# Four normalisations ahead of a weight load on GpSimd, one v load behind w_out, and two w_out jobs swapped, in a sliding-window attention + gated MLP kernel

## The chip, the cores and the metric

One core of one Trainium2 chip runs the whole program. The metric is the device time of one execution in microseconds, as the median over runs; lower is better.

The engines are named as in the profile: PE is TensorE (matmuls; PEld is its weight load), DVE is VectorE, ACT is ScalarE, POOL is GpSimd, SP is SyncE, which only issues DMAs here. POOL issues DMAs too, and each of its requests occupies POOL while the descriptors are written.

## The reference

q, k and v are 8 batches x 8 heads x 576 positions x 64. Attention is causal with a window of 64 positions. Its output, laid out as 4608 tokens x 512, goes through a two-layer network.

```python
def _attn_ref(q, k, v):
    scores = scale * np.matmul(q, k.transpose(0, 1, 3, 2))
    mask = (rel >= 0) & (rel < window)          # rel = query position - key position, window = 64
    scores = np.where(mask, scores, -1000000000.0)
    attn = softmax(scores)
    return np.matmul(attn, v)

def _moe_ref(x, w_in, w_out):                   # x 4608 x 512, w_in 512 x 2048, w_out 2048 x 512
    h = x @ w_in
    g = h * np.cos(h)
    return g @ w_out
```

(The softmax is abridged. Inputs are float32; the kernel loads them as bfloat16 and writes float32.)

## The kernel before

The 4608 tokens are worked on in 9 tiles of 512. Batch 0 fills tile 0 and the first 64 tokens of tile 1, and so on. Per tile there is attention (scores, softmax, transposition of the weights, values), which gives `xT`; then `h = w_in x xT` in 16 blocks, `gT = h * sin(h + pi/2)`, and `out = gT x w_out`. From tile 1 on a planner weaves the attention of later batches into the network of the current tile. Tile 0 and the attention of batch 1 have no earlier network to hide behind: their order is written out by hand, in a string of steps called `FIRST`, and each engine runs its instructions in the order in which the steps were written. The change is in this string alone.

A step is a letter code and arguments. Those that matter here:

- `Lwi.i` and `Lwo.i` load quarter i of w_in and w_out (lines 208 and 211, POOL requests); `Lv1.c` loads chunk c of v of batch 1 (line 192); `Lq1.p`, `Lk1.p` load heads of batch 1, `Lq2.c`, `Lk2.c` chunks of batch 2 (lines 169 and 186).
- Scores are made in groups. For tile 0 a group is (p, g): head pair p, half g of the tile; the groups `G*.8` to `G*.18` are the rest of batch 0 and batch 1. Each group runs `s` (scores on PE), `m` (row maximum on DVE), `e` (exponential with its sum on ACT, line 376), `i` (reciprocal `rden` on DVE, line 386), `n` (normalisation `w = e * rden`, line 393, on POOL unless its letter is `d`), and `w` (transposition on PE, line 409) with `c` (copy of the transposed weights to `wT`). For batch 1, `Gc` is the transposition by a DMA that SP issues (line 412), `Gw` the one on PE.
- `zA`, `zB`, `zC` spread v of batch 0 to the in-between block positions: `zA` on DVE, `zB` and `zC` as DMAs of SP (line 203). `yA`, `yB` do it for batch 1 on POOL, and `y.1.d` on DVE.
- `v.a.g` are the value matmuls of two head pairs for half g (line 446), `x` their copy to `xT`, `h.g.f` the w_in matmuls of two blocks for half g (line 460), `V.p` and `X.p` the same two steps of tile 1 (line 428).
- `o.j.m` multiplies the four blocks of w_out's quarter j into output block m of tile 0 (line 479): four matmuls, one job. `oc.m` copies the finished output block out of PSUM.

An `h.g.f` with f = 2, 3 reads w_in's second quarter (`Lwi.1`), f = 4, 5 the third (`Lwi.2`), f = 6, 7 the fourth. All requests of POOL go through one software DMA queue.

Of the kernel before, what the change touches and what calls it, by code (L numbers as in the profile page):

```python
# [10 lines left out]
def _safe_warn(msg, *a, **kw):  # L11
# [37 lines left out]


FIRST = (
# [19 lines left out]
)  # L71


# [713 lines left out]
```

## Time and profile before

| | us |
|---|---|
| median of 3 runs (297.42 to 297.9) | 297.88 |
| the profiled execution, its own time | 296.92 |
| its span, first to last instruction | 295.2 |
| PE busy in the span | 285.3 (97%) |
| ACT, DVE, POOL busy | 238.0, 230.3, 209.7 |
| software DMA queue: packets' time as a share of 16 engines' span | 83.5% |

Something of 1.72 us lies around the span in the profiled execution, and the median of the runs is 0.96 us above that execution. TensorE's granted clock is 1.000 throughout. Since PE is busy 97% of the span, what counts is where PE stands still, and which wait ends last there. Times in the timeline rows are microseconds from the start of the span: start, duration, engine, line, operation, count, and in brackets the idle time ahead of it with what ended it.

### The profile page before, as it was taken

To read this page: it belongs to the slowest core of one execution; us is meant where nothing else is said; L and a number is where in the kernel's file an instruction comes from. 1 tells how busy PE (TensorE), PEld (TensorE's weight loads), DVE (VectorE), ACT (ScalarE), POOL (GpSimd) and SP (SyncE) were. 2 spreads that over 40 slices of the span, in tenths; PEclk is the share of its full clock that TensorE was granted. 3 is DMA by queue.
4 is the path that set the end of the run, shared out by engine and by line. 5 is a ranking of instruction groups with operands and counts; after the bars stand their busy time and mean duration, and the time that the engine had idled before them with its cause. 6 is when DMAs were issued, how large, how long until landed. Compare 5 with 4: busy or idle time off the path is not lost.

```text
span 295.2 us, 8262 instructions
## 1 busy us (share of the span) xinstructions
PE 285.3 (97%) x2786; PEld 163.2 (55%) x2815; DVE 230.3 (78%) x906; ACT 238.0 (81%) x791; POOL 209.7 (71%) x230
## 2 busy tenths in 40 slices
PE   8979999999999999999999999999999999999995
PEld 3668854544454444444454545444547854884595
DVE  4998888887887876788678876996689878957853
ACT  5998699888987798879987999799977896937710
POOL 9999568992899759984999399948995476133200
PEclk9999999999999999999999999999999999999999
DMA  7999999999999999999999999999959415042013
GB/s 149 174 201 205 196 191 143 141 143 155 203 197 120 162 235 154 155 163 232 168 142 158 235 155 145 147 213 185 141 122 200 45 38 178 2 117 83 0 38 107
DMA packets 168267, 43.81 MB, mean 148 GB/s; under 512 B 155616, under 2 KB 163872, under 8 KB 168224
## 3 DMA queue, kind: packets, MB, share of 16 engines
q0 software_dynamic: 100896, 18.06, 83.5%
q1 hardware_dynamic: 67184, 25.15, 46.7%
q8 instruction: 22, 0.36, 0.5%
q14 instruction: 21, 0.17, 0.2%
q10 hardware_dynamic: 144, 0.07, 0.1%
HBM read 36.70 MB, written 9.44 MB: 156 GB/s over the span
## 4 chain that ended last, share of the span: by engine, by line
PE 86%; POOL 5%; ACT 3%; DMA 2%; issue 2%; DVE 1%; POOLq 0%
PE h_ps L496 38%; PE out_ps L747 18%; PE out_ps L585 13%; PE h_ps L460 5%; PE out_ps L479 5%; PE o_ps L428 3%; ACT e L376 2%; PE s_ps L327 2%; DMA wT<-w 2%; POOL v L192 1%; POOL q L169 1%; POOL k L169 1%; POOL w L393 1%; PE tw_ps L409 1%; PE s_ps L349 1%
## 5 line engine op out<-in xcount | busy, mean ns | idle before, releaser
L496 PE MATMUL h_ps<-xT,w_in 128*128 128x512 bf16 x502 | 111.3, 379 | 1.3 <-DVE xT L130 0.8
L393 POOL TENSOR_TENSOR w<-e,rden 128x512 bf16<-128x512 f32 (+1 forms) x68 | 69.2, 1030 | 48.6 <-DVE rden L386 38.6
L734 DVE TENSOR_TENSOR gT<-h_ps,sin 128x512 bf16<-128x512 f32 x128 | 84.6, 687 | 21.8 <-ACT sin L731 20.4
L376 ACT ACTIVATE e<-s,negm 128x128 f32<-128x128 f32 (+1 forms) x256 | 97.2, 382 | 2.6 <-DVE negm L364 1.6
L731 ACT ACTIVATE sin<-h_ps 128x512 f32<-128x512 f32 x128 | 73.6, 599 | 25.4 <-PE h_ps L496 23.5
L496 PEld LDWEIGHTS <-w_in 128*128 128x128 bf16 x512 | 50.2, 98 | 59.3
L747 PE MATMUL out_ps<-w_out,gT 128*128 128x512 bf16 x305 | 68.7, 379 | 1.1 <-issue 0.8
L364 DVE CUSTOM_DVE_ANT_0 s<-s_ps,mask 128x128 f32<-128x128 f32 (+1 forms) x256 | 55.8, 277 | 1.9 <-PE s_ps L349 1.6
L747 PEld LDWEIGHTS <-gT 128*128 128x128 bf16 x320 | 30.4, 98 | 35.5
L376 ACT ACTIVATION_READ_ACCUMULATOR e<-s,negm 128x1 f32 x256 | 48.0, 188 | 0.0
L192 POOL DMA_DIRECT2D v<-in_v_dram x40 | 34.1, 874 | 1.0 <-issue 0.9
L186 POOL DMA_DIRECT2D q<-in_q_dram x30 | 26.3, 894 | 3.6 <-issue 3.0
L186 POOL DMA_DIRECT2D k<-in_k_dram x30 | 26.3, 887 | 0.0
L386 DVE RECIPROCAL rden<-den 128x4 f32<-128x4 f32 (+1 forms) x73 | 12.0, 165 | 17.2 <-ACT e L376 16.8
L130 POOL COPY v<-v 64x1536 bf16<-64x1536 bf16 (+3 forms) x16 | 22.9, 1431 | 0.4
L364 DVE DVE_READ_ACCUMULATOR2_ANT negm<- 128x1 f32 x256 | 21.2, 83 | 0.0
L525 POOL TENSOR_TENSOR qT<-gT 128x512 bf16<-128x512 bf16 x12 | 13.6, 1154 | 9.1 <-DVE gT L734 9.0
L130 DVE CAST xT<-o_ps 128x512 bf16<-128x512 f32 x24 | 15.5, 680 | 5.8 <-PE o_ps L428 5.5
L585 PEld LDWEIGHTS <-gT 128*128 128x128 bf16 x152 | 14.0, 98 | 2.2
L460 PE MATMUL h_ps<-xT,w_in 128*128 128x256 bf16 x128 | 14.6, 273 | 0.0
L479 PE MATMUL out_ps<-w_out,gT 128*128 128x512 bf16 x60 | 14.3, 380 | 0.3 <-issue 0.2
L556 DVE TENSOR_TENSOR out_sb<-out_ps,p 128x512 f32<-128x512 f32 (+2 forms) x16 | 8.6, 548 | 6.7 <-ACT p L130 5.6
(90 smaller groups left out, 327.0 us busy)
## 6 DMA issues: line engine op xcount, KB each, us to landing
out_dram<-out_sb SPq DMA_DIRECT2D x16, 512.0 KB, 8.2
v<-in_v_dram POOLq DMA_DIRECT2D x32, 128.0 KB, 5.8
q<-in_q_dram POOLq DMA_DIRECT2D x24, 128.0 KB, 8.5
k<-in_k_dram POOLq DMA_DIRECT2D x24, 128.0 KB, 7.1
w_in<-in_moe_w_in_dram POOLq DMA_DIRECT2D x4, 512.0 KB, 9.4
w_out<-in_moe_w_out_dram POOLq DMA_DIRECT2D x4, 512.0 KB, 11.0
q<-in_q_dram POOLq DMA_DIRECT2D x7, 144.0 KB, 5.7
k<-in_k_dram POOLq DMA_DIRECT2D x7, 144.0 KB, 5.8
```

What stands on the lines that cost most here:

```text
L130: {"a": nc.scalar.copy, "p": nc.gpsimd.tensor_copy}.get(engine, nc.vector.tensor_copy)(out, in_)
L186: nc.gpsimd.dma_start(out=st[name, b][0:n, c].rearrange("p (h d) -> p h d", h=H), in_=src.rearrange("h p d -> p h d"))
L192: nc.gpsimd.dma_start(out=vt.rearrange("p (h d) -> p h d", h=H), in_=v[b, :, c * 128:c * 128 + n, :].rearrange("h p d -> p h d"))
L364: nc.vector.tensor_tensor_reduce(out=s[:, u, c], in0=s_ps[:, u, c], in1=mask[:, 2 - j % 2 if j else 0, c], scale=-scale if b else -1.0, sc ...
L376: nc.scalar.activation(e[:, u, c], s[:, u, c], AF.Exp, bias=negm[:, u:u + 1], scale=1.0 if n < n_first else -1.0, accum_out=den[:, u:u + 1])
L393: (nc.gpsimd if engine == "p" else nc.vector).tensor_tensor(out=w[:, 0:u], in0=e[:, 0:u], op=ALU.mult, in1=rden[:, 0:u].unsqueeze(2).to_br ...
L460: nc.tensor.matmul(out=h_ps[:, half * e:half * e + half], lhsT=w_in_sb[:, ks, ff * 128:ff * 128 + 128], rhs=st["xT", 0][:, ks, half * g:ha ...
L496: nc.tensor.matmul(out=st["h", ff], lhsT=w_in_sb[:, ks, ff * 128:ff * 128 + 128], rhs=st["xT", mt][:, ks], start=start, stop=stop)
L585: nc.tensor.matmul(out=to[n_] if split else to[:, e], lhsT=lhs[name][f // 2][:, f % 2, 128 * e:128 * e + 128], rhs=rhs[name][:, f, lo:hi], ...
L731: nc.scalar.activation(sin, h_ps, AF.Sin, bias=math.pi / 2.0)
L734: nc.vector.tensor_tensor(out=gt[:, e], in0=h_ps, in1=sin, op=ALU.mult)
L747: nc.tensor.matmul(out=o_ps[e], lhsT=gT[ff // 2][:, ff % 2, ms * 128:ms * 128 + 128], rhs=w_out_sb[:, ff], start=ff == 0, stop=ff == n_ff - 1)
```

## The change

Four edits in the string of steps; no function changes, and after it the file is one line shorter, so that its line numbers are lower by one.

```diff
-e.3.0 Lwi.2 Tk.1 n.1.0.p s.2.1.1 Pq.1.d Gs.10.2 m.2.1 Gs.9.4 n.0.0.p Pk.1.a n.2.0.p i.3.0 e.1.1 w.0.0 zA.0.d w.1.0 c.0.0.d Gs.12.0 w.2.0 n.3.0.p i.0.1 c.1.0.d zA.1.d
+e.3.0 Tk.1 n.1.0.p s.2.1.1 Pq.1.d zA.0.d Gs.10.2 Gs.9.4 n.0.0.p Pk.1.a n.2.0.p e.1.1 w.0.0 w.1.0 c.0.0.d i.3.0 Gs.12.0 w.2.0 n.3.0.p Lwi.2 i.0.1 c.1.0.d m.2.1 zA.1.d
...
-h.1.3.1 Lv1.0 Lwo.1 ... Lwo.3 h.1.7.4 Lv1.1
+h.1.3.1 Lwo.1 ... Lwo.3 h.1.7.4 Lv1.0 Lv1.1
...
-o.0.1.2 Gi.9 o.2.0 ... o.1.1 ... o.3.0 Ge.13 o.2.1 Gi.11 oc.0.d
+o.0.1.2 Gi.9 o.1.1 ... o.2.0 ... o.2.1 Ge.13 o.3.0 Gi.11 oc.0.d
```

1. `Lwi.2` goes from ahead of the norms of tile 0's first half to behind them.
2. On DVE, `zA.0` goes ahead of the maximum `m.2.1`, which moves behind `c.1.0`, and `i.3.0` behind `c.0.0`.
3. `Lv1.0` goes from ahead of `Lwo.1` to behind `Lwo.3`.
4. Of the output jobs, `o.1.1` changes places with `o.2.0`, and `o.2.1` with `o.3.0`: the third and the fourth quarter of w_out are first read one job later.

On POOL, the first norms of tile 0 stand behind the third w_in request before the change (a name in brackets is a semaphore that the instruction waits for; DMASW0 to DMASW7 are eight completion counters that POOL's requests use in turn, so that each request waits for the one eight places ahead of it):

```order
L208 DMA w_in<-in_moe_w_in_dram 128x4x512 [waits DMASW7_49]
L208 DMA w_in<-in_moe_w_in_dram 128x4x512 [waits DMASW0_49]
L393 TENSOR_TENSOR w<-e,rden 128x512 [waits DVE_49,Pool_49]
L393 TENSOR_TENSOR w<-e,rden 128x512
L393 TENSOR_TENSOR w<-e,rden 128x512 [waits DVE_49] x5
L208 DMA w_in<-in_moe_w_in_dram 128x4x512 [waits DMASW1_49]
```

Now the third request (the one on DMASW0) is behind four of them:

```order
L207 DMA w_in<-in_moe_w_in_dram 128x4x512 [waits DMASW7_49]
L392 TENSOR_TENSOR w<-e,rden 128x512 [waits DVE_49,Pool_49]
L392 TENSOR_TENSOR w<-e,rden 128x512
L392 TENSOR_TENSOR w<-e,rden 128x512 [waits DVE_49] x2
L207 DMA w_in<-in_moe_w_in_dram 128x4x512 [waits DMASW0_49]
L392 TENSOR_TENSOR w<-e,rden 128x512 [waits DVE_49] x3
L207 DMA w_in<-in_moe_w_in_dram 128x4x512 [waits DMASW1_49]
```

The four norms moved up by one request; the three behind it did not.

Also on POOL, later, around the w_out requests and up to the first norm of batch 1 (w with 384 columns is group 10), before:

```order
L192 DMA v_78<-in_v_dram 128x8x64 [waits DMASW6_49]
L211 DMA w_out<-in_moe_w_out_dram 128x4x512 [waits DMASW7_49]
L169 DMA k<-in_k_dram 96x2x384 [waits DMASW0_49]
L211 DMA w_out<-in_moe_w_out_dram 128x4x512 [waits DMASW1_49]
L211 DMA w_out<-in_moe_w_out_dram 128x4x512 [waits DMASW2_49]
L192 DMA v_78<-in_v_dram 128x8x64 [waits DMASW3_49]
...
L192 DMA v_77<-in_v_dram 64x8x64 [waits DMASW6_49]
L186 DMA q<-in_q_dram 128x8x64 [waits DMASW7_49,PE_49]
L186 DMA q<-in_q_dram 128x8x64 [waits DMASW0_49]
L186 DMA q<-in_q_dram 128x8x64 [waits DMASW1_49]
L393 TENSOR_TENSOR w<-e,rden 128x384 [waits DVE_49,PE_49,Pool_49]
```

and now:

```order
L210 DMA w_out<-in_moe_w_out_dram 128x4x512 [waits DMASW6_49]
L168 DMA k<-in_k_dram 96x2x384 [waits DMASW7_49]
L210 DMA w_out<-in_moe_w_out_dram 128x4x512 [waits DMASW0_49]
L210 DMA w_out<-in_moe_w_out_dram 128x4x512 [waits DMASW1_49]
L191 DMA v_78<-in_v_dram 128x8x64 [waits DMASW2_49]
...
L191 DMA v_77<-in_v_dram 64x8x64 [waits DMASW6_49]
L185 DMA q<-in_q_dram 128x8x64 [waits DMASW7_49,PE_49]
L185 DMA q<-in_q_dram 128x8x64 [waits DMASW0_49]
L185 DMA q<-in_q_dram 128x8x64 [waits DMASW1_49]
L392 TENSOR_TENSOR w<-e,rden 128x384 [waits DVE_49,PE_49,Pool_49]
```

With the v request gone from ahead of them, the last three w_out requests and the k request moved to the counter before their old one; the q requests stay on DMASW7, 0 and 1. So the counter DMASW1 that the third q request waits for is that of w_out's third quarter before, and of its fourth quarter now.

On DVE, in the first half of tile 0, before:

```order
L130 COPY qT1_76<-tq_ps_386 128x576
L359 TENSOR_REDUCE negm_460<-s_ps_441 128x4
L386 RECIPROCAL rden_476<-den_420 128x4
L130 COPY v0_77<-v0_77 64x512
L130 COPY wT_495<-tw_ps_484 128x512
L386 RECIPROCAL rden_512<-den_348 128x4
L130 COPY wT_514<-tw_ps_490 128x512
```

and now:

```order
L129 COPY qT1_76<-tq_ps_386 128x576
L129 COPY v0_77<-v0_77 64x512
L129 COPY wT_490<-tw_ps_480 128x512
L385 RECIPROCAL rden_492<-den_420 128x4
L385 RECIPROCAL rden_510<-den_348 128x4
L129 COPY wT_512<-tw_ps_485 128x512
L358 TENSOR_REDUCE negm_514<-s_ps_440 128x4
```

The maximum (`m.2.1`) left its place ahead of the first copy of v and stands two copies of `wT` later; the reciprocal of `den_420` (`i.3.0`, for the fourth norm) follows the first copy of `wT`.

37 rows, old and new, of the table FIRST are left out of this document.

## The prediction, before the changed kernel was run

> **What bounds the kernel now.** I read the page's chain of work that ended last, then PE's waits and timeline between 10 and 56 us, where the change lies, and then, for each place where PE could start earlier, the engine or transfer that it would meet next.
>
> ```profile
> span 295.2 us, 8262 instructions
> PE 86%; POOL 5%; ACT 3%; DMA 2%; issue 2%; DVE 1%; POOLq 0%
> PE tw_ps L409 <- POOL w L393: 1.4, 2, 1.1
> ```
>
> PE is most of the chain, so a microsecond counts only if PE stands still for it. In the stretch of the change POOL's norms cost PE 1.4 us in two waits. The rows, with what follows them on PE:
>
> ```profile
> 16.65 0.62 PE L409 MATMUL tw_ps<-ident,w 128*128 128x128 bf16 x8 [1.06 <-POOL w L393]
> 18.73 0.40 PE L409 MATMUL tw_ps<-ident,w 128*128 128x128 bf16 x4 [0.38 <-POOL w L393]
> 24.43 0.44 PE L446 MATMUL o_ps<-wT,v 128*64 128x64 bf16 x16 [0.17 <-issue]
> 26.37 10.65 PE L460 MATMUL h_ps<-xT,w_in 128*128 128x256 bf16 x96
> ```
>
> The norms are late because POOL first writes three w_in requests:
>
> ```profile
> 11.95 1.52 POOL L208 DMA_DIRECT2D w_in<-in_moe_w_in_dram  x2
> 13.74 0.74 POOL L208 DMA_DIRECT2D w_in<-in_moe_w_in_dram  x1 [0.27 <-DVE rden L386]
> 14.55 6.16 POOL L393 TENSOR_TENSOR w<-e,rden 128x512 bf16<-128x512 f32 x6
> 13.42 0.17 DVE L386 RECIPROCAL rden<-den 128x4 f32<-128x4 f32 x1
> 16.42 0.18 DVE L386 RECIPROCAL rden<-den 128x4 f32<-128x4 f32 x1 [0.34 <-ACT e L376]
> 19.54 0.66 ACT L130 CAST xT<-o_ps 128x512 bf16<-128x512 f32 x1
> ```
>
> **Part 1: the third w_in request behind four norms, and the DVE moves.** POOL is free at 11.95 + 1.52 = 13.47, and the first norm's reciprocal ends at 13.42 + 0.17 = 13.59. So the norms start at about 13.65 instead of 14.55: 0.90 us earlier. A norm takes 6.16 / 6 = 1.03 us. The fourth needs i.3.0, whose exponentials bound it to 16.4 (the row that waits for ACT); its new place behind c.0.0 puts it at about 16.5, still ahead of the fourth norm's turn at 13.65 + 3 x 1.03 = 16.75. So PE's two waits would end at about 15.75 and 17.84. The DVE moves cost nothing: zA.0 and c.0.0 are done before 16.75, and m.2.1 feeds exponentials that ACT cannot start before its earlier ones are through. If that cover fails, it is the next exponential that is late, by one row maximum.
>
> At 17.78 POOL writes the third request (0.74 us), and the fifth norm starts at about 18.59, where it started before (14.55 + 4 x 1.03 = 18.67). So the gain is 0.90 us for the first half alone, and ACT's first copy to xT, at 19.54 behind its exponentials, hardly moves. PE then needs what the DMA queue brings. Two kinds of row tell when that is: issue on POOL or SP, and the time from issue to landing. In order: the three w_in requests above (11.95, 12.7, 13.74), then the second SP request that spreads v (zB.1) with its landing:
>
> ```profile
> w_in<-in_moe_w_in_dram POOLq DMA_DIRECT2D x1, 512.0 KB, 8.3
> w_in<-in_moe_w_in_dram POOLq DMA_DIRECT2D x1, 512.0 KB, 10.4
> w_in<-in_moe_w_in_dram POOLq DMA_DIRECT2D x1, 512.0 KB, 12.5
> 18.27 0.84 SPq L203 DMA_DIRECT2D v<-v  x1
> v<-v SPq DMA_DIRECT2D x1, 128.0 KB, 6.1
> ```
>
> The quarters land at 20.25, 23.1 and 26.24, one about every 3.0 us: the queue serves them one after the other and has a backlog, so a request's own issue time doesn't set its landing. The third, issued at 17.78, is still queued 5.3 us before the second lands, and should land at 26.24 as before. Its first reader is the w_in matmul at 26.37. And zB.1 lands at 18.27 + 6.1 = 24.37; the value matmuls at 24.43, with 0.17 us of idle PE that the row calls issue, are v.0.1, which read that spread. PE thus waits for a transfer there already. The front gain of 0.90 us ends at 24.37 at the latest, and at 26.24 once more: I take 0 for what is left, between a bound of 0.1 (26.37 less 26.24) and no loss.
>
> A rule speaks against this move: the Trainium skill, "DMA: Bandwidth & Descriptors", section "Rules for kernel authors", says to issue a DMA early and to wait for it late. Read as landing following issue, the third quarter would come 17.78 - 13.74 = 4.04 us later, at 30.28, and PE would stand 3.9 us, for 301.8. The spacing of the landings contradicts that here; it stays as a rival.
>
> **Part 2: Lv1.0 behind w_out, the swapped jobs, and the counters.** No wait for w_out appears among PE's, so the swapped jobs remove none; they cost nothing as long as the finished block's copy out of PSUM, one job later, is through before its bank's next scores, two jobs on; without that cover the price would be the rest of one copy. What the move of Lv1.0 does change is which transfer POOL's third q request waits for. POOL's requests that wait for a counter show the pattern:
>
> ```profile
> 23.99 0.80 POOL L211 DMA_DIRECT2D w_out<-in_moe_w_out_dram  x1
> w_out<-in_moe_w_out_dram POOLq DMA_DIRECT2D x1, 512.0 KB, 7.7
> 31.94 0.74 POOL L211 DMA_DIRECT2D w_out<-in_moe_w_out_dram  x1 [2.08 <-DMA w_out<-in_moe_w_out_dram]
> 29.09 0.76 POOL L211 DMA_DIRECT2D w_out<-in_moe_w_out_dram  x1
> w_out<-in_moe_w_out_dram POOLq DMA_DIRECT2D x1, 512.0 KB, 12.0
> 41.37 0.88 POOL L186 DMA_DIRECT2D q<-in_q_dram  x1 [0.59 <-DVE negm L364]
> ```
>
> The fourth w_out request, eight behind the first, starts at 31.94, 0.25 us after the first lands (23.99 + 7.7 = 31.69). The third q request starts at 41.37, 0.28 us after w_out's third quarter lands (29.09 + 12.0 = 41.09); the row names DVE, but the order shows only a counter. Now that counter is the fourth quarter's. Its landing:
>
> ```profile
> w_out<-in_moe_w_out_dram POOLq DMA_DIRECT2D x1, 512.0 KB, 11.7
> 26.05 0.63 POOL L169 DMA_DIRECT2D q<-in_q_dram  x1
> q<-in_q_dram POOLq DMA_DIRECT2D x1, 144.0 KB, 7.8
> 26.67 0.92 POOL L192 DMA_DIRECT2D v<-in_v_dram  x1
> v<-in_v_dram POOLq DMA_DIRECT2D x1, 128.0 KB, 8.1
> ```
>
> Issued at 31.94, it lands at 43.64. Lv1.0 took the queue from 26.05 + 7.8 = 33.85 to 26.67 + 8.1 = 34.77, so without it the quarter lands 0.92 us earlier, at 42.72, and the third q request starts at 43.0: 1.63 us later than before. Queued behind it on POOL are all norms of batch 1; who waits for them are PE's transposition of group 8 and SP's DMA transpositions:
>
> ```profile
> 42.26 4.55 POOL L393 TENSOR_TENSOR w<-e,rden 128x384 bf16<-128x384 f32 x5
> 46.75 1.03 POOL L130 COPY v<-v 64x1024 bf16<-64x1024 bf16 x1
> 48.62 1.04 POOL L393 TENSOR_TENSOR w<-e,rden 128x512 bf16<-128x512 f32 x1 [0.83 <-DVE rden L386]
> 50.64 1.03 POOL L393 TENSOR_TENSOR w<-e,rden 128x512 bf16<-128x512 f32 x1
> 52.17 0.55 PE L409 MATMUL tw_ps<-ident,w 128*128 128x128 bf16 x7
> 53.74 1.28 PE L428 MATMUL o_ps<-wT,v 128*64 128x64 bf16 x64
> 45.75 1.86 SPq L412 DMA_TRANSPOSE wT<-w  x1
> 49.02 1.65 SPq L412 DMA_TRANSPOSE wT<-w  x1
> 50.76 1.22 SPq L412 DMA_TRANSPOSE wT<-w  x1
> wT<-w SPq DMA_TRANSPOSE x1, 2.9
> ```
>
> The five norms and the copy shift by 1.63 and end at 46.75 + 1.03 + 1.63 = 49.41. The norm at 48.62 waited for its reciprocal, so 0.83 of the delay is taken up there and 49.41 - 48.62 = 0.79 passes on. The norm of group 8 ends at 50.64 + 1.03 + 0.79 = 52.46 instead of 51.67. PE came to it at 52.17, and would now find it at 52.5: a new wait of 0.35 us. That is the first term.
>
> The second is SP. Its six transpositions run back to back; the last is issued at 50.76 and lands at 53.66. The chain begins 1.63 later, and part of that comes back only if its long ones (1.86, 1.65) shrink to the 1.22 of the last, 1.07 in all: the last is issued between 50.76 + 1.63 - 1.07 = 51.3 and 52.4, and lands 2.9 later, between 54.2 and 55.3. Its reader is the third of the four value products, a half into the row at 53.74 + 0.35, at 54.73. So the term lies between 0 and 0.6; I take 0.1, since the early end goes with the DMA load of the stretch, which is past by then.
>
> **The sum** against the profiled execution: 296.92 + 0 (front) + 0.35 + 0.1 = 297.37, a change of +0.45. The runs' median stands 0.96 above that execution, so the forecast is 297.88 + 0.45 = 298.3. About 0.2%, 0.6 us, is what a measurement of this kernel can tell from no change; the forecast lies inside it.
>
> **Rivals.**
>
> A (forecast): POOL's q request waits for w_out's fourth quarter, PE pays 0.2 to 0.6: 298.1 to 298.5. Chance 0.45.
>
> B: the same, but the last DMA transposition is late by up to its bound, and PE waits there for 0.3 to 0.8 more: 298.5 to 299.2. For it speaks that the transpositions at 45.75 and 49.02 were slow while the v chunks were still arriving; against it, that these are past by then. Chance 0.22.
>
> C: nothing reaches PE. The fourth quarter would have to land 0.35 us earlier than I reckon, at 42.37. It competes with SP's first transposition at its end, which now starts later, so some of that is possible. 297.7 to 298.1. Chance 0.10.
>
> D, faster: the transfers share the queue instead of following each other. Then taking the third w_in request out of it from 13.74 to 17.78 makes the first two and the v spread land earlier, and PE keeps its 0.90: 297.0, to 297.3 where a third is lost. It decides if zB.1 lands at 23.5 rather than 24.37. The landings 3.0 us apart speak against it; that the v spread, from SP's own queue, landed between two of them (24.37 between 23.1 and 26.24) speaks for some of it. Chance 0.17. The Trainium skill gives the same outcome by another way: "DMA: Bandwidth & Descriptors", "Anatomy of one DMA — SWDGE (gpsimd) path", fits one DMA as 2.0 us plus bytes over 436 GB/s, an estimate of 3.2 us for 512 KB; no quarter would then be late. This trace has 8.3 to 12.5 us.
>
> E, much slower: the third quarter lands with its issue, not with the queue. 299.2 to 301.8 (the price above, 3.9, as the far end). Chance 0.06.
>
> **How the numbers follow.** A is the likeliest, 298.3, with 298.1 to 298.5 as its own range. The range 297.2 to 299.2 takes in A, B, C and a third of D; it leaves out the rest of D and E, under 2 in 10. Slower by over 0.2% is over 298.48: B and E, 0.28. Faster is under 297.28: D, 0.17. The same: A and C, 0.55.
>
> **What would show it.** In the changed trace: the first norm on POOL near 13.65, and PE's first transposition near 15.75 (part 1); v.0.1 still at 24.4 and the 96 w_in matmuls still from 26.3; the third q request near 43.0 and the first norm of batch 1 behind it; a PE wait on POOL's norm at about 52.5; and the value products' wait on a DMA, or none. I am wrong if v.0.1 starts before 24, if the q request starts at 41.4, or if PE waits for w_in.

## The result, and the profile after

The change made the kernel slower: 300.71 us as the median of its runs against 298.19 for the kernel before in the same comparison, a ratio of 1.0069 with a 95% interval of [1.0043, 1.0095]. The forecast was 298.3 with a range up to 299.2, so the direction of its small loss was right and the size was not: the ratio is worth 2.1 us, the forecast said 0.45. Executions of one kernel scatter here by 2 to 7 us, whichever kernel it is, and the ratios leave out the longest of them, so that they are not the quotients of the medians. What a single profile shows is taken for the time only where other profiles bear it out.

The profiled execution of the changed kernel took 301.61 us, 4.69 more than that of the kernel before. Its page: the span, and the chain of work that ended last, by engine (of before: 295.2, and PE 86%, POOL 5%, ACT 3%, DMA 2%).

```profile
span 299.8 us, 8291 instructions
PE 81%; DMA 7%; ACT 5%; DVE 2%; POOL 2%; issue 1%; SPq 0%; POOLq 0%; DVEq 0%
```

POOL's share of the chain went down, and DMA's went from 2% to 7%. PE's waits in the changed kernel (engine, line, what it waited for: us in total, times, longest) name which transfers:

```profile
PE o_ps L427 <- DMA wT<-w: 3.2, 3, 2.5
PE o_ps L445 <- ACT sin L465: 1.2, 1, 1.2
PE tk_ps L224 <- DMA k<-in_k_dram: 1.1, 1, 1.1
PE tw_ps L408 <- POOL w L392: 0.9, 2, 0.6
```

Before, the last of these was the largest of the stretch, 1.4 in all. The first was 0.5, in two waits near 117 us and none in the stretch; now 2.5 of its 3.2 us are one piece, PE's wait for SP's last DMA transposition of batch 1, and the rest is again far behind the stretch, near 121 us. The timelines of POOL, SP and PE in the changed kernel show how it came to that. First the requests and norms on POOL, then SP's six transpositions and the last one by itself with its time to landing, then PE:

```profile
41.24 0.87 POOL L185 DMA_DIRECT2D q<-in_q_dram  x1 [0.47 <-DMA w_out<-in_moe_w_out_dram]
43.77 0.87 POOL L185 DMA_DIRECT2D q<-in_q_dram  x1 [1.66 <-DMA w_out<-in_moe_w_out_dram]
44.66 4.45 POOL L392 TENSOR_TENSOR w<-e,rden 128x384 bf16<-128x384 f32 x5
52.30 1.03 POOL L392 TENSOR_TENSOR w<-e,rden 128x512 bf16<-128x512 f32 x1
53.28 1.62 POOL L185 DMA_DIRECT2D q<-in_q_dram  x2
45.53 9.34 SPq L411 DMA_TRANSPOSE wT<-w  x6
53.65 1.22 SPq L411 DMA_TRANSPOSE wT<-w  x1
wT<-w SPq DMA_TRANSPOSE x1, 5.0
53.83 0.55 PE L408 MATMUL tw_ps<-ident,w 128*128 128x128 bf16 x7
55.40 0.81 PE L427 MATMUL o_ps<-wT,v 128*64 128x64 bf16 x34
58.73 0.66 PE L427 MATMUL o_ps<-wT,v 128*64 128x64 bf16 x30 [2.53 <-DMA wT<-w]
```

The third q request waits 1.66 us for w_out's fourth quarter and starts at 43.77, 0.28 us after that quarter landed; it was to be 43.0. The five norms follow at 44.66 instead of 42.26, and SP's chain at 45.53 instead of 43.13. The last transposition is issued at 53.65, behind the first of POOL's next two q requests (53.28), and lands 5.0 us later, at 58.65. Before, it was issued at 50.76, ahead of both (51.62), and landed 2.9 later.

The front of the changed kernel, POOL, then DVE, then PE:

```profile
12.15 1.53 POOL L207 DMA_DIRECT2D w_in<-in_moe_w_in_dram  x2
14.07 3.04 POOL L392 TENSOR_TENSOR w<-e,rden 128x512 bf16<-128x512 f32 x3 [0.39 <-DVE rden L385]
17.75 1.04 POOL L392 TENSOR_TENSOR w<-e,rden 128x512 bf16<-128x512 f32 x1 [0.65 <-DVE rden L385]
16.11 1.14 DVE L129 COPY v<-v 64x512 bf16<-64x512 bf16 x1 [0.30 <-DMA v<-in_v_dram]
17.18 0.41 DVE L129 COPY wT<-tw_ps 128x512 bf16<-128x512 bf16 x1
18.84 0.40 PE L408 MATMUL tw_ps<-ident,w 128*128 128x128 bf16 x4 [0.60 <-POOL w L392]
26.09 0.44 PE L445 MATMUL o_ps<-wT,v 128*64 128x64 bf16 x16 [1.18 <-ACT sin L465]
28.03 2.14 PE L459 MATMUL h_ps<-xT,w_in 128*128 128x256 bf16 x18
```

The first three norms are earlier, the fourth is not: it waits for a reciprocal that stands on DVE behind `zA.0`'s copy, which ran for 1.14 us. The matmuls at 26.09 (`v.0.1`) read the spread of v. The row names ACT, but they start 0.09 us after the second request of the spread has landed, as they do at 24.43 before and in every profile in which PE waits there. Those at 28.03 stood at 26.37 before: PE is 1.66 us late as it leaves the front, and at the group-8 transposition it still is (53.83 against 52.17). By the scores that follow the value products it is 4.38 late (59.33 against 54.95), so 2.72 of the 4.69 arose in between, and 2.53 of them are the wait for the transposition. The 1.66 is within the scatter of `v.0.1`, which starts at 24.43 to 26.11 over all profiles; the wait is what returns in several of them.

### The profile page after: what moved, and what is told of

It reads as the page before. It is cut to its first block, busy times and chain, and to the rows that moved or that the text cites. A ratio compares the mean times of both kernels' runs of the same rounds, so it can differ in the third digit from the quotient of the medians.

```text
span 299.8 us, 8291 instructions
## 1 busy us (share of the span) xinstructions
PE 288.7 (96%) x2815; PEld 163.5 (55%) x2815; DVE 230.5 (77%) x906; ACT 238.0 (79%) x791; POOL 209.5 (70%) x230
## 4 chain that ended last, share of the span: by engine, by line
PE 81%; DMA 7%; ACT 5%; DVE 2%; POOL 2%; issue 1%; SPq 0%; POOLq 0%; DVEq 0%
PE h_ps L495 37%; PE out_ps L746 19%; PE out_ps L584 12%; PE h_ps L459 4%; ACT e L375 3%; DMA wT<-w 3%; PE o_ps L427 3%; PE out_ps L478 3%; PE s_ps L326 2%; DMA v<-in_v_dram 2%; DMA q<-in_q_dram 2%; DVE v L129 1%; POOL w L392 1%; PE s_ps L348 1%; DVE s L363 0%
## 5 line engine op out<-in xcount | busy, mean ns | idle before, releaser
L746 PE MATMUL out_ps<-w_out,gT 128*128 128x512 bf16 x320 | 72.0, 379 | 0.0
L478 PE MATMUL out_ps<-w_out,gT 128*128 128x512 bf16 x64 | 14.8, 380 | 0.0
```

The costliest lines, as they stand in the source:

```text
L746: nc.tensor.matmul(out=o_ps[e], lhsT=gT[ff // 2][:, ff % 2, ms * 128:ms * 128 + 128], rhs=w_out_sb[:, ff], start=ff == 0, stop=ff == n_ff - 1)
```

## The experiments

Theory A: with the v load moved, POOL's third q request waits on the completion counter of w_out's fourth quarter; batch 1's norms and SP's transpositions are late by that, so that the last transposition loses a race: it is issued beside or behind POOL's next q and k requests, and lands about 2 us late. Its rivals: the loss is in the front (the DVE moves, the w_in request); it is the traffic of the moved load and of w_out, wherever the q request stands; or SP's late chain alone.

**The change in parts.** The first kernel has edits 1 and 2 only (the w_in request and the DVE moves), the second edit 3, the third edit 4, the fourth is the changed kernel once more.

```diff
-"e.3.0 Lwi.2 Tk.1 n.1.0.p s.2.1.1 Pq.1.d Gs.10.2 m.2.1 Gs.9.4 n.0.0.p Pk.1.a n.2.0.p i.3.0 e.1.1 w.0.0 zA.0.d ... n.3.0.p i.0.1 c.1.0.d zA.1.d"
+"e.3.0 Tk.1 n.1.0.p s.2.1.1 Pq.1.d zA.0.d Gs.10.2 Gs.9.4 n.0.0.p Pk.1.a n.2.0.p e.1.1 w.0.0 ... c.0.0.d i.3.0 ... n.3.0.p Lwi.2 i.0.1 c.1.0.d m.2.1 zA.1.d"
```

> Edits 1 and 2 alone (w_in's third request behind four norms, and the three DVE moves). Theory A, both halves of the change cost: v's first spread on DVE (zA.0) waits for its chunk and for POOL's norm, c.0.0 starts no earlier than 17.1, v.0.1 on PE starts near 26 and the whole is 1 to 1.7 us slower than before. Theory B, the loss is in the second half alone and the late front in the profile is scatter of the DMAs: within 0.4 us of before, v.0.1 near 24.4. Theory C, the front gains as it was meant to: 0.3 to 0.9 us faster.

```diff
-"h.1.3.1 Lv1.0 Lwo.1 ... h.1.7.4 Lv1.1"
+"h.1.3.1 Lwo.1 ... h.1.7.4 Lv1.0 Lv1.1"
```

> Edit 3 alone (batch 1's first v load behind w_out). Theory A: the third q request waits for w_out's fourth quarter and starts near 43.0, the six DMA transpositions start near 44.8, the last one lands after 56, PE waits 1 to 2.5 us for it in the value products; 1 to 2.5 us slower. Theory B: the same, and this is all of the loss. Theory C, the recorded forecast: the q request at 43.0 too, but PE waits only 0.3 to 0.6 us.

```diff
-"o.2.0 Ge.14 Gn.10.p Gm.13 Gc.10 Gi.12 o.1.1"
+"o.1.1 Ge.14 Gn.10.p Gm.13 Gc.10 Gi.12 o.2.0"
...
-"o.3.0 Ge.13 o.2.1"
+"o.2.1 Ge.13 o.3.0"
```

> Edit 4 alone (the two swapped pairs of output jobs). All theories: within 0.3 us of before, PE's rows the same; if the finished block's copy were late for its bank, PE would wait before the scores of group 17, near 46.5, and the whole be 0.3 to 0.7 us slower.

The whole change has the diff shown above.

> The changed kernel once more, on the chip of the three parts. Theory A: 1.5 to 4 us slower than before, and about the sum of the parts; the wait for the DMA transposition is there again in its profile (1 us or more), the late v.0.1 too. Theory B: the wait for the transposition is there, v.0.1 is at 24.4 to 24.8. Scatter between executions is expected to be larger than that of before, since PE now waits for transfers.

| kernel | median us | ratio to before |
|---|---|---|
| before | 298.06 | |
| edits 1 and 2 | 298.38 | 1.0028 [0.9998, 1.0059] |
| edit 3 | 300.11 | 1.0068 [1.0035, 1.01] |
| edit 4 | 298.09 | 1.0014 [0.9986, 1.0041] |
| all four | 300.4 | 1.0074 [1.0039, 1.0109] |

Edit 3 alone costs what the whole change costs. The swapped output jobs cost nothing that can be told, and the front at most little. (One execution of edits 1 and 2 took 596.33 us; it is in the median and not in the ratio.) The eight times of edit 3 alone are three from 297.46 to 298.28 and five from 299.4 to 302.59, and four of them are over 300 us, where the kernel before has 3 of 26. Its profiled execution, 297.46, is the shortest. There the counter's wait is present and the late transposition is not. POOL's request, the last transposition with its landing, and POOL's next requests:

```profile
42.88 0.87 POOL L186 DMA_DIRECT2D q<-in_q_dram  x1 [1.66 <-DVE negm L364]
51.63 1.22 SPq L412 DMA_TRANSPOSE wT<-w  x1
wT<-w SPq DMA_TRANSPOSE x1, 3.1
53.02 1.62 POOL L186 DMA_DIRECT2D q<-in_q_dram  x2
```

So the counter's 1.66 us alone cost PE next to nothing in that execution; something else decides. (The row names DVE, but the request starts 0.3 us after w_out's fourth quarter has landed, 13.3 us after its issue at 29.26, as it did behind the third quarter in the kernel before.) The first and the fourth kernel were profiled in long executions, 301.65 and 301.12, and in both PE waits for the transposition, 2.3 and 1.8 us. In the first, which doesn't have edit 3, the counter cost only 0.60 us; there one of SP's six transpositions held the chain for 3.3 us, and the last came 0.27 us behind POOL's request. So the counter is not the only way to lose that race, and with edit 3 the long executions are more frequent. TensorE's granted clock doesn't explain the long executions: it was 0.999 in the changed kernel's at 301.61, and 0.994 in edit 4's at 298.24.

**Taking the counter's wait away.** In the next two kernels the third q request stands behind the norm of group 8, so that w_out's fourth quarter is not waited for ahead of the norms (the second q request still waits 0.7 us for the third): once with edit 3 alone, once with the whole change. In the third, edit 3 is made shorter: the v load goes behind w_out's third quarter instead of its fourth, so that the q request's counter is that of the v load and the fourth quarter stands one counter further on.

```diff
-"Lq2.1 Lq2.2 o.0.1.2"
+"Lq2.1 o.0.1.2"
...
-"Gn.8.p Lq2.3 Lq2.4"
+"Gn.8.p Lq2.2 Lq2.3 Lq2.4"
```

> Batch 1's first v load behind w_out, alone, as in the run of that edit, and the third q request moved behind the norm of group 8, beside the fourth: POOL then waits for no w_out quarter between the second q request (about 40.4) and its first norm of batch 1. Theory A (the counter delays batch 1's norms, SP's last DMA transposition is issued later by that, and PE waits about 2 us for it in executions where it is issued behind POOL's next q request): the norms start near 42.0 or earlier, the last transposition is issued near 50.5 and ahead of POOL's next q request, PE waits under 0.7 us for it, and the ratio to the kernel before is 0.998 to 1.002. Theory B (the later v load or the w_out loads without it, as traffic, make PE late wherever the q request stands): 1.005 to 1.009, as with that edit alone (1.0068). Theory C (the place of the q requests in the queue alone decides): PE waits for the q tile or for the transposition behind three requests in a row, 1.003 or more, with the last transposition behind the first of the three.

> The whole change, and the third q request moved behind the norm of group 8. Theory A: most of the loss goes: 1.000 to 1.003, with no wait over 0.7 us for a DMA transposition; what stays is the front's (the DVE moves), up to 0.003. Theory B: 1.005 to 1.009 as the whole change has. A rival that puts the loss at the front (zA.0 ahead of the row maximum, later first copies): 1.005 or more with no wait at the transposition.

```diff
-"h.1.3.1 Lv1.0 Lwo.1 ... h.1.6.2 Lwo.2 g.0.7"
+"h.1.3.1 Lwo.1 ... h.1.6.2 Lwo.2 Lv1.0 g.0.7"
```

> Batch 1's first v load only two POOL requests later than before: behind w_out's third quarter instead of its fourth. The third q request's counter is then that v load's, which should land near 41.1 as w_out's third quarter did in the kernel before, so the q request starts near 41.4, and the traffic is nearly that of the edit alone. Theory A: norms of batch 1 start near 42.3 as before, no wait over 0.7 us for a transposition, ratio 0.999 to 1.002. Theory B (the traffic): 1.004 to 1.009.

| kernel | median us | ratio to before (298.13) |
|---|---|---|
| edit 3, q request behind group 8 | 297.83 | 0.9989 [0.9959, 1.0018] |
| all four, q request behind group 8 | 298.24 | 0.9993 [0.9964, 1.0022] |
| v load behind w_out's third quarter | 298.1 | 0.9998 [0.997, 1.0025] |

All three are back at the time of before, and together they speak against the traffic: in the first the v load and the w_out quarters stand exactly where edit 3 puts them, and in the third the q requests stand where edit 3 leaves them; what both take away is the counter's wait for w_out's fourth quarter. In the third's profile the second and third q requests run together, where the kernels with edit 3 have a gap of 1.66 us between them:

```profile
41.10 1.75 POOL L186 DMA_DIRECT2D q<-in_q_dram  x2 [0.73 <-DMA w_out<-in_moe_w_out_dram]
42.85 4.57 POOL L393 TENSOR_TENSOR w<-e,rden 128x384 bf16<-128x384 f32 x5
```

The whole change at 0.9993 also bounds the front: its edits are in that kernel, and with the transposition on time no loss above 0.0022, 0.7 us, is left by its interval.

**The race by itself.** With edit 3 alone, the norm of group 15 goes from DVE to POOL, ahead of the fourth and fifth q requests, which are 1.3 to 1.7 us later by that; the counter's wait stays.

```diff
-"Gn.8.p Lq2.3 Lq2.4 o.2.2 o.3.2 o.1.3 Gn.16.d Gi.15 Gn.15.d"
+"Gn.8.p o.2.2 o.3.2 o.1.3 Gn.16.d Gi.15 Gn.15.p Lq2.3 Lq2.4"
```

> Batch 1's first v load behind w_out, alone, and the norm of group 15 on POOL instead of DVE, ahead of the fourth and fifth q requests, which start about 1.3 us later by that (near 54.3 instead of 53.0). The counter wait ahead of batch 1's norms stays (third q request near 43). Theory A's race (PE waits for the last transposition if it is issued behind POOL's next q request): the transposition, issued at 51.6 to 53.7, is then always ahead; no wait over 0.9 us for it, and the ratio is 1.000 to 1.003. A rival, that the delay of SP's chain alone makes the transposition late whatever POOL issues: the wait stays at 1.5 to 2.5 us in executions of the long kind and the ratio at 1.005 to 1.009.

And edit 3 alone was profiled again, now in a long execution, 301.21:

> Batch 1's first v load alone, once more, for a profile of a long execution (over 300, some half of its runs). In a long one theory A expects PE's wait of 1.8 to 2.5 us at the last DMA transposition, issued behind POOL's fourth q request; or, if it is ahead, the same size of wait at batch 2's last transposition of k (near 78 to 81), which the run with group 15's norm on POOL showed. In a short one (under 298.5) neither wait is above 0.7. Rival: a long execution has neither, and its time lies in waits spread over later passes.

The two profiles make a pair. In each, the last transposition, POOL's next requests and the landing; first edit 3 alone in the long execution, with PE's wait:

```profile
52.75 1.23 SPq L412 DMA_TRANSPOSE wT<-w  x1
52.72 1.62 POOL L186 DMA_DIRECT2D q<-in_q_dram  x2
wT<-w SPq DMA_TRANSPOSE x1, 5.0
57.83 0.66 PE L428 MATMUL o_ps<-wT,v 128*64 128x64 bf16 x30 [2.42 <-DMA wT<-w]
```

and the same with group 15's norm ahead of those requests:

```profile
52.71 1.22 SPq L412 DMA_TRANSPOSE wT<-w  x1
54.38 1.62 POOL L186 DMA_DIRECT2D q<-in_q_dram  x2
wT<-w SPq DMA_TRANSPOSE x1, 2.5
```

The transposition is issued at the same time within 0.04 us. With POOL's requests beside it, it takes 5.0 us and PE stands 2.42; with them 1.67 us behind it, it takes 2.5 and PE doesn't stand. The DMA queues from 54.5 to 56.5 us show what ran meanwhile (queue: packets, MB, share of 16 engines; q0 carries POOL's requests, q1 SP's). The long execution of edit 3 alone:

```profile
q0 software_dynamic: 1387, 0.17, 137.0%
q1 hardware_dynamic: 402, 0.10, 24.9%
```

and with group 15's norm ahead of the requests, where POOL's queue moved nothing in that time:

```profile
q1 hardware_dynamic: 981, 0.24, 64.2%
```

In the first, packets of POOL's queue run from 54.65 on, and the 16 updates of the transposition's semaphore come between 56.06 and 57.79; in the second they come from 55.01 to 55.19, and POOL's packets start at 56.75. So a late chain on SP alone isn't the cause, and what POOL has issued is. The Trainium skill, "DMA: Bandwidth & Descriptors", section "Issuing engines are not separate DMA queues", says that DMAs of all issuing engines run on the same 16 DMA engines and interleave. The trace agrees: 2.5 us without POOL's packets, 5.0 with them.

The expected time of that kernel was missed all the same: 300.09 us, 1.0067 [1.0033, 1.0101], where theory A had 1.000 to 1.003. PE's wait in that profile was elsewhere:

```profile
80.91 0.41 PE L327 MATMUL s_ps<-kT,qT 64*64 64x128 bf16 x8 [2.44 <-DMA kT<-k]
```

POOL's loads of batch 2 were later by the norm put ahead of them, and the DMA transposition of batch 2's k came 2.44 us late for its scores. It was issued at 72.05, against 71.64 in the long execution of edit 3, and landed 8.7 us later instead of 6.9. My reading, not shown by a run of its own, is that the delay of POOL's queue was only handed on: it has two readers with little room, one at 54 and one at 78 to 81, and the norm bought room for the first out of that of the second.

**The race provoked, in the kernel before.** The fourth q request goes ahead of a v copy and of group 8's norm, so that it is issued ahead of the last transposition.

```diff
-"Gn.13.p yB.p Gc.11 Gn.8.p Lq2.3 Lq2.4"
+"Gn.13.p Lq2.3 yB.p Gc.11 Gn.8.p Lq2.4"
```

> The kernel before, with one thing moved: POOL's fourth q request goes ahead of the second v copy and the norm of group 8, so it is issued near 49.7, about 1 us ahead of SP's last DMA transposition (near 50.8), whose own inputs stay on time. Theory A's race (a transposition issued behind POOL's next loads lands late): it lands 4 to 5 us after its issue instead of 2.9, near 55.2, and PE waits 0.8 to 1.5 us for it; the norm of group 8 is later by one request and PE waits 0.3 to 0.9 for it: ratio 1.003 to 1.007. Rival (the transposition is late only where SP's chain itself was late, and what POOL has issued plays no part): it lands in 2.5 to 3.2 us, PE waits only for the norm, 0.3 to 0.9, ratio 1.000 to 1.003.

It took 299.09 against 298.02, 1.0048 [1.0018, 1.0079], within what theory A expected; its times spread from 297.74 to 301.47, as those of the kernels do that lose the race at times, and one more stands apart at 756.39. Its profiled execution was one of the shortest (297.8) and has neither wait, but the race was lost in it: the request was issued at 49.95, the transposition at 50.18, POOL's packets run from 52.41 to 53.92, and the last of the 16 updates of the transposition's semaphore comes at 54.80, 4.6 us after the issue instead of 2.9. PE came to the third value product only at 55.11 (54.35 in the kernel before), so that it found the transposition landed. So the late landing is provoked with SP's chain on time, as theory A has it and its rival doesn't; what the median's 1.0048 consists of, this profile doesn't show.

**Two candidates.** The kernel before with the third q request behind group 8's norm, and the same with the w_in request moved too (edit 1 without the DVE moves).

```diff
-"Lq2.1 Lq2.2 o.0.1.2"
+"Lq2.1 o.0.1.2"
...
-"Gn.8.p Lq2.3 Lq2.4"
+"Gn.8.p Lq2.2 Lq2.3 Lq2.4"
```

> A candidate: the kernel before with only the third q request moved behind the norm of group 8, so that batch 1's norms wait for no w_out quarter. Norms start near 41.0 to 41.5 instead of 42.26, the last DMA transposition is issued near 50 and has the most lead before POOL's next loads. If the slow executions of the kernel before (over 300) are those in which it loses that race, they go, and the ratio of the medians is 0.997 to 0.999; if not, 0.999 to 1.001, since PE waits only 0.5 us there in the profiled execution.

It has 298.72 against 298.02, 1.0013 [0.9985, 1.004]: no gain.

```diff
-"e.3.0 Lwi.2 Tk.1 n.1.0.p"
+"e.3.0 Tk.1 n.1.0.p"
...
-"n.3.0.p i.0.1"
+"n.3.0.p Lwi.2 i.0.1"
```

> A candidate: the kernel before with only POOL's orders changed, the third w_in request behind four norms and the third q request behind the norm of group 8; DVE's order, the v load and the output jobs stay. If the DVE moves are what used up the earlier norms (zA.0 held POOL and DVE back), the first norm starts near 13.65, the fourth ends near 17.8 without a wait on DVE, the spread of v is issued no later than 17.5 and the ratio is 0.996 to 0.999. If the queue and the spread's landing set the end of the front whatever DVE does (the forecast's term of 0), it is 0.999 to 1.002, with PE's wait moved to v.0.1 near 24.4 to 25.8. PE waits under 0.7 us for the last DMA transposition by theory A.

It has 298.33 against 297.84, 1.0012 [0.9985, 1.0038]: no gain either. Its front is close to what the forecast of part 1 had described. Four norms on POOL, the spread of v on SP, PE's first transposition, the value matmuls:

```profile
13.96 4.09 POOL L393 TENSOR_TENSOR w<-e,rden 128x512 bf16<-128x512 f32 x4
17.61 2.46 SPq L203 DMA_DIRECT2D v<-v  x3
16.05 0.62 PE L409 MATMUL tw_ps<-ident,w 128*128 128x128 bf16 x8 [0.25 <-POOL w L393]
26.11 0.44 PE L446 MATMUL o_ps<-wT,v 128*64 128x64 bf16 x16 [1.74 <-ACT sin L466]
```

Without the DVE moves the four norms run without a gap, and PE's waits for them fall from 1.4 us in all to 0.3. All of it is lost again at `v.0.1`, which waits 1.74: the row names ACT, but the matmuls start 0.09 us after the spread's second request, which landed 7.6 us after its issue here, at 26.02. No version that was run is faster than the kernel before beyond its interval.

All profiles side by side, in us: the issue of the last transposition of batch 1, POOL's request for q that comes next to it, the time from issue to landing, and PE's wait at the third value product, which reads it:

| kernel | transposition issued | POOL's q request | landed after | PE waited |
|---|---|---|---|---|
| before | 50.76 | 51.62 | 2.9 | none |
| edit 4 | 51.04 | 52.94 | 3.8 | none |
| edit 3, short execution | 51.63 | 53.02 | 3.1 | none |
| edit 3, q behind group 8 | 50.64 | 52.58 | 3.3 | none |
| all, q behind group 8 | 50.74 | 52.68 | 2.5 | none |
| v load behind third quarter | 51.37 | 52.23 | 2.9 | none |
| edit 3, group 15 on POOL | 52.71 | 54.38 | 2.5 | none |
| before, q behind group 8 | 51.42 | 53.36 | 2.7 | none |
| before, q behind group 8 and w_in behind norms | 51.37 | 53.31 | 2.4 | none |
| race provoked | 50.18 | 49.95 | 4.6 | none |
| edits 1 and 2 | 52.44 | 52.17 | 4.9 | 2.3 |
| edit 3, long execution | 52.75 | 52.72 | 5.0 | 2.4 |
| all four, again | 53.15 | 53.11 | 4.7 | 1.8 |
| all four | 53.65 | 53.28 | 5.0 | 2.5 |

In every profile in which the transposition leads by 0.8 us or more it lands within 3.8 and PE doesn't stand for it; in every one in which it doesn't, it takes 4.6 to 5.0, and PE stands 1.8 to 2.5, but for the provoked race, where PE came late itself. (For two rows, the provoked race and the one above it, the landing is the last of the semaphore's 16 updates.)

## Why the prediction was wrong, step by step

- **The counter (part 2): right.** The third q request was to start at 43.0, and starts at 43.77 and 43.27 in the two profiles of the changed kernel and at 42.88 and 43.49 in the two of edit 3 alone. With the v load two places earlier the wait is gone.
- **The norm of group 8 (first term, 0.35): not seen as a term.** The norm ended at 53.33 in the profiled execution, against 52.46 forecast, but PE came to its transposition only at 53.83, late from the front, and no row shows a wait there. In the long execution of edit 3 alone the norm ended at 52.77 and PE was there at 52.82, again without a wait that the rows show. No profile shows the term, and it is not what cost the time.
- **The last DMA transposition (second term): this is the step that failed.** The forecast gave it 0.1, with 0.6 as its end, from an issue between 51.3 and 52.4 and the landing of 2.9 that the kernel before showed, "since the early end goes with the DMA load of the stretch, which is past by then". Two numbers were off. The issue came at 51.63 to 53.65, and the landing grew to 4.7 to 5.0, because the quiet stretch had been measured where the transposition led POOL's next seven requests by 0.86 us (50.76 against 51.62). A delay of 1.63 uses that lead up. The requests are POOL's and follow the norm of group 8, to which the forecast passed on only 0.79 of the delay; so by its own numbers the lead was anything from 1.1 us to none (51.3 to 52.4 for the transposition, 51.62 + 0.79 = 52.41 for the request), and it priced only the case with lead. In the four profiles that lose the race with PE on time the term measured 1.8 to 2.5 us of waiting, where the kernel before has none; the ratio of the whole change is worth 2.1, over executions of which some lose the race and some don't.
- **Rival B had the place and too small a price**: 0.3 to 0.8 more, for a transposition that is late by its own delay and takes no longer.
- **The front (term 0): right in the sum, wrong in one cover.** The gain of the earlier norms does end at the spread of v, as forecast: with four norms in a row PE gave back 1.74 us at `v.0.1`. But "the DVE moves cost nothing: `zA.0` and `c.0.0` are done before 16.75" failed. `zA.0` was put on DVE where its v chunk had not landed (0.30 us) and where POOL was just starting a norm, and its copy took 1.14 us. The kernel before has the same copy at 16.52, 0.07 us before a norm of POOL ended, and its sister `zA.1` at 17.93, 0.74 us before the next one did:

```profile
16.52 0.26 DVE L130 COPY v<-v 64x512 bf16<-64x512 bf16 x1
17.93 0.89 DVE L130 COPY v<-v 64x512 bf16<-64x512 bf16 x1
```

  So in the changed kernel `c.0.0` came at 17.18, `i.3.0` behind it, and the fourth norm started at 17.75 instead of 16.75. The Trainium skill, "SBUF — State Buffer", section "Who interferes with whom", has a rule for it: VectorE in its modes with two ports, which a copy can use, and GpSimd contend for one pair of ports, and whichever issues first blocks the other until it is done. The trace agrees: the copy ended 0.14 us after the norm that ended at 17.11, and those of the kernel before 0.18 and 0.15 us after theirs. In the time of the whole it cost nothing that can be told (0.9993 with all four edits and the transposition on time).
- **The spread's landing at 24.37 was taken as fixed, and isn't.** `v.0.1`, which reads it, starts anywhere from 24.43 to 26.11 over the profiles, with edit 3 alone (whose front is that of before) at 25.82 and 24.87. The 1.66 us that the profiled execution lost in the front is within that. What makes the spread early or late was not settled.
- **The sum** was +0.45 and the ratio says 2.1: the second term was short by some 2 us in the executions that lose the race, and nearly right in the others, as far as they were profiled.
- **Rivals D and E fell.** The third w_in quarter, issued at 18.73, landed 7.7 us later, at 26.43, by the queue and not by its issue; so the norms' gain was neither kept (D) nor turned into a wait for w_in (E).

## What to carry to other kernels

A landing time read from a trace holds for the traffic that stood beside it: before moving a transfer, look for the next requests of every queue and count the lead over them, because the price is not the delay but what the transfer costs once the lead is gone. A request that waits for a completion counter is tied to the request a fixed number of places ahead, so moving any load in between changes which transfer the following work waits for; list the counters of the requests just ahead of compute on the issuing engine. And where the executions of one kernel spread widely, profile a short one and a long one: the difference between them points to the race.

## What the runs showed of the hardware

- Batch 1's last DMA transposition of SP took 2.4 to 3.8 us to land when it led POOL's next requests by 0.8 us or more, and 4.6 to 5.0 when it did not, at the same size; between a lead of 0.86 us and a lag of 0.03 no profile lies. What decides in one and the same kernel whether SP's chain keeps its lead was not settled: from first issue to the last one's end the six took 8.2 to 10.0 us over the profiles.
- A bfloat16 copy of 64 x 512 on DVE from SBUF to SBUF that begins while a norm is running on POOL ends 0.14 to 0.18 us after that norm does (six copies in three profiles), so that the same copy took anything from 0.26 to 1.14 us.
- Request to landing for 512 KB of weights was 7.7 us for the moved third quarter and 12.5 in its old place: issued 5 us later, it landed at nearly the same time (26.43 against 26.24).
